# Storing the result of a decode block in two transfers from two engines

## The chip, the core and the metric

The kernel runs on one core of a Trainium2 chip. The metric is the time of one execution on the device in microseconds (us), as a median of several runs; one further execution is recorded by the hardware profiler.

## What is computed

A decode step for a batch of 4 tokens with 448 features: attention over the last 1024 entries of a cache with 8 heads of keys and values and 16 of queries, then a channel MLP, each with a residual.

```python
def _A_ref(x, k_cache, v_cache, wq, wo):
    q = (x @ wq).reshape(B, Sq, Hq, Dh).transpose(0, 2, 1, 3)
    k = jnp.repeat(k_cache[:, :, Sk - W:, :], rep, axis=1)
    v = jnp.repeat(v_cache[:, :, Sk - W:, :], rep, axis=1)
    scores = jnp.einsum("bhqd,bhkd->bhqk", q, k) * (Dh ** -0.5)
    o = jnp.einsum("bhqk,bhkd->bhqd", _softmax(scores, axis=-1), v)
    return o.transpose(0, 2, 1, 3).reshape(B, Sq, Hq * Dh) @ wo

def _B_ref(x, w1, b1, w2, b2):
    y = _layernorm(x, axis=-1)
    h = _gelu(jnp.einsum("bsd,df->bsf", y, w1) + b1)
    return jnp.einsum("bsf,fd->bsd", h, w2) + b2

h = x + _A_ref(_layernorm(x), A_k_cache, A_v_cache, A_wq, A_wo)
h2 = h + _B_ref(_layernorm(h), B_w1, B_b1, B_w2, B_b2)
```

## The kernel before

The cache and the weights, some 88 MB in float32, are packed on the host into large arrays of 128 rows. SyncE loads them one after another into a ring of three slots; each slot is loaded again when TensorE has read the last of what it held. TensorE works through the heads as the loads arrive: queries from `wq`, scores against the keys, a softmax with VectorE and ScalarE, values, and the output weights. The last slots hold the weights of the MLP, `w1` and `w2`, which arrive in pieces of falling size.

No operation is issued where it is written. `Machine` (line 79) stands in for the engines and records every call as an `Op` (line 58), in the order of the program. `emit` (line 132) then works out from the parts of the tensors that each `Op` reads and writes which earlier ones it needs, drops the needs that others imply, and issues all of them with waits on semaphores, from line 165 on. In the trace every operation therefore has the line of the recorder (L75). An `Op` with `dma` set gets a semaphore of its own, `landed_i`, that its transfer raises by 16; the others count up the semaphore of their engine. Line 61 sets `dma` for whatever is on SyncE ("SP"). Line 178 ends the program: SyncE waits for the last `Op` on the list.

The end of the kernel is a straight line. The second weights' products are summed into the bank `py` by TensorE over lines 707 to 725, with VectorE and ScalarE only bringing `gT` and `pas` along; line 727 adds the residual and bias `hb` on VectorE and puts 128 rows of 128 floats into `res`; line 728 stores `res` to `out` in one transfer of 64 KB that SyncE issues. Each group of 32 rows holds a quarter of the features, and 4 rows of a group are the batch's tokens; the host picks those out.

Of the kernel before, what the change touches and what calls it, by code (L numbers as in the profile page):

```python
# [16 lines left out]
P = 128  # L17
H = P // 2
# [16 lines left out]
class Memory:  # L35


    def __init__(self, shape, psum):
        self.psum = psum
        self.row = 1 if psum else int(np.prod(shape[1:]))  # L40
        self.granules = 1 if psum else -(-shape[0] // GRANULE)
        self.wrote = np.full((self.granules, self.row), -1)
        self.read = {}
# [14 lines left out]
class Op:  # L58
    def __init__(self, engine, emit, outs, ins, own):
        self.engine, self.emit, self.outs, self.ins, self.own = engine, emit, outs, ins, own  # L60
        self.dma = engine == "SP"


class Engine:
# [14 lines left out]
class Machine:  # L79
# [52 lines left out]
    def emit(self):  # L132
        ops = self.ops
        who = [("DMA", i) if op.dma else op.engine for i, op in enumerate(ops)]
        at_start = [None] * len(ops)
        seen = {}
        waits = []
        for i, op in enumerate(ops):
            clock = dict(seen.get(op.engine, {}))
            needs = sorted(self._needs(i, op), reverse=True)  # L140
            if op.engine == "PE":
                needs = [j for j in needs if ops[j].engine != "PE"]
            taken = []
            for j in needs:
                if clock.get(who[j], -1) >= j:
                    continue
                taken.append(j)
                for key, value in list(at_start[j].items()) + [(who[j], j)]:
                    clock[key] = max(clock.get(key, -1), value)
            kept = []  # L150
            for j in taken:
                others = [k for k in taken if k != j]
                if not any(who[k] == who[j] and k > j or at_start[k].get(who[j], -1) >= j for k in others):
                    kept.append(j)
            waits.append(sorted(kept))
            at_start[i] = clock
            seen[op.engine] = clock
        waited = {j for w in waits for j in w}
        counter = {n: self.nc.alloc_semaphore(f"done_{n}") for n in self.issuer if n != "SP"}
        count = dict.fromkeys(counter, 0)  # L160
        mark = {}
        for i, op in enumerate(ops):
            marks = [mark[j] for j in waits[i]]
            issuer = self.issuer[op.engine]
            alone = op.own == "matmul" and op.ins[0].dtype == BF16
            for sem, value in marks if alone else marks[:-1]:
                issuer.wait_ge(sem, value)
            done = op.emit()
            if marks and not alone:
                done.wait_op(*marks[-1], "sem-ge")  # L170
            if op.dma:
                mark[i] = (self.nc.alloc_semaphore(f"landed_{i}"), 16)
                done.then_inc(mark[i][0], 16)
            elif i in waited:
                count[op.engine] += 1
                mark[i] = (counter[op.engine], count[op.engine])
                done.then_inc(counter[op.engine], 1)
        self.nc.sync.wait_ge(*mark[len(ops) - 1])


class Pool:
# [19 lines left out]
def block_kernel(nc, wq0, k0, wq1, l1, l2, l3, l4, l5, l6, l7, l8, k7, vo, v7, wo, w1, w2, out):  # L201
    real, nc = nc, Machine(nc)
# [53 lines left out]
    def output_weights(t):  # L256
# [6 lines left out]
        out=ident, in_=ident, compare_op=ALU.not_equal, fill=1.0, base=0, pattern=[[-1, P]], channel_multiplier=1  # L263
# [356 lines left out]
    def w1_part(a, j):  # L620
        if a < 3:
            return slice(0, P), w1t[3 if a == 2 else a][:, FQ * j : FQ * (j + 1)]
        rows = slice(H * (j // 2), H * (j // 2) + H)
        return rows, w1t[2][rows, FQ * (j % 2) : FQ * (j % 2 + 1)]
# [46 lines left out]
    for a in (0, 1, 3, 2):  # L671
        m = Q if a == 0 else B
        for j in range(4):
            rows, w = w1_part(a, j)
# [50 lines left out]
            )  # L725
    res = once.tile([P, P], F32, tag="res", name="res")
    nc.vector.tensor_add(res, py.rearrange("p i c -> p (i c)"), hb)
    nc.sync.dma_start(out, res)
    nc.emit()


# [77 lines left out]
```

## Time and profile before

| what | us |
|---|---|
| median of 3 runs | 212.09 |
| lowest and highest of them | 211.88, 212.33 |
| the profiled execution, its own time | 211.87 |
| its span, from the first to the last instruction | 210.6 |
| TensorE busy | 139.0 |
| VectorE busy | 28.8 |
| ScalarE busy | 14.4 |

All 212.09 us are one core's. The difference between the profiled execution's own time and its span, 1.27 us, lies ahead of the first and behind the last instruction of the trace. Times inside the trace are counted from the start of the span. A row of the timeline gives the start, the length, the engine, the line, the operation with what it writes and reads, how many of them are merged, and in brackets the idle time before it and what ended that. "SPq" is SyncE's queue: its rows are the issues of transfers, and a transfer goes on after its issue ends.

### The profile page before, as it was taken

The page shows a single profiled execution, that of the slowest core. Times are in us where ns is not written, and L with a number is a line of the kernel's source. Part 1 is how long each engine was busy: PE and PEld are TensorE (multiplying, and loading weights), DVE is VectorE, ACT ScalarE, POOL GpSimd, SP SyncE. Part 2 cuts the span into 40 slices and gives each one's busy share as a digit, 9 for nine tenths or more (in the row PEclk, how much of TensorE's full clock was granted, in tenths as well). Part 3 has the DMA queues.
Part 4 walks back from the last instruction along what each step waited for, and adds up shares of the span by engine and source line. Part 5 has one row for each costly group of instructions (what it writes and reads, how often), then busy time and mean ns, then how long its engine had stood idle before and what let it go on. Part 6 is the DMA issues. An engine that isn't in the chain of part 4 may idle for free.

```text
span 210.6 us, 2206 instructions
## 1 busy us (share of the span) xinstructions
PE 139.0 (66%) x984; PEld 47.2 (22%) x984; DVE 28.8 (14%) x135; ACT 14.4 (7%) x34; POOL 5.0 (2%) x17
## 2 busy tenths in 40 slices
PE   0467759621971679198359775419806999888996
PEld 0420202200220223034012222102301233224332
DVE  7210101300020011013001104000100213012320
ACT  2010000200000010020000002000100002010311
POOL 5100000000000000000000000000000000000100
PEclk9999996996799559969967999757965899999999
DMA  7999999899999999999999999999999999999993
GB/s 296 429 399 473 448 492 389 386 436 507 398 398 410 531 389 410 410 519 398 413 411 448 481 398 425 434 470 398 434 411 442 416 428 429 425 407 439 424 409 138
DMA packets 3400, 88.42 MB, mean 420 GB/s; under 512 B 512, under 2 KB 768, under 8 KB 1344
## 3 DMA queue, kind: packets, MB, share of 16 engines
q1 hardware_dynamic: 3392, 88.30, 97.6%
q8 instruction: 7, 0.11, 0.2%
q14 instruction: 1, 0.01, 0.0%
HBM read 88.23 MB, written 0.07 MB: 419 GB/s over the span
## 4 chain that ended last, share of the span: by engine, by line
DMA 77%; PE 18%; SPq 2%; DVE 1%; issue 1%; ACT 0%
DMA slot<-l 64%; DMA slot<-w 14%; PE b_o L75 9%; PE b_s L75 4%; PE b_acc L75 3%; SPq L75 2%; PE b_m L75 1%; DVE oT L75 1%; DVE w_o L75 0%; PE b_t L75 0%; DVE o_u L75 0%; ACT o_u L75 0%; DVE o_res L75 0%
## 5 line engine op out<-in xcount | busy, mean ns | idle before, releaser
L75 PE MATMUL b_o<-slot,pT 128*32 128x512 f32 x224 | 33.6, 752 | 29.3 <-DMA slot<-l 28.5
L75 PE MATMUL b_s<-slot,qT 128*32 128x512 f32 x256 | 36.6, 722 | 10.4 <-DMA slot<-l 9.1
L75 PE MATMUL b_m<-slot,yT 128*32 128x512 f32 (+1 forms) x76 | 11.9, 734 | 11.5 <-DMA slot<-l 6.4
L75 PEld LDWEIGHTS b_o<-slot,pT 128*32 128x32 f32 x224 | 7.8, 132 | 51.4 <-DMA slot<-l 30.9
L75 PE MATMUL b_t<-idle 128*32 128x512 bf16 x64 | 18.1, 404 | 0.5 <-DVE pT L75 0.5
L75 PEld LDWEIGHTS b_s<-slot,qT 128*32 128x32 f32 x256 | 8.8, 128 | 35.9 <-issue 22.5
L75 ACT ACTIVATE o_p<-b_s,w_nm 128x512 f32<-128x512 f32 x8 | 5.4, 682 | 93.1 <-DVE w_nm L75 93.1
L75 DVE TENSOR_REDUCE w_mx<-b_s 128x1 f32<-128x512 f32 x8 | 5.5, 692 | 43.7 <-PE b_s L75 43.7
L75 DVE TENSOR_SCALAR w_o<-b_o,w_rec 128x512 f32<-128x512 f32 x4 | 3.0, 751 | 52.5 <-PE b_o L75 52.5
L75 PEld LDWEIGHTS b_m<-slot,yT 128*32 128x32 f32 x76 | 4.3, 142 | 17.9 <-DMA slot<-l 6.9
L75 PEld LDWEIGHTS b_t<-idle 128*32 128x32 bf16 x64 | 5.9, 100 | 10.3 <-issue 5.8
L75 DVE TENSOR_REDUCE w_sm<-b_m 128x32 f32<-128x128 f32 x4 | 1.2, 291 | 48.2 <-PE b_m L75 48.2
L75 PE MATMUL b_t<-ident,o_p 128*128 128x128 f32 x32 | 5.0, 285 | 4.0 <-ACT o_p L75 3.9
L75 PE MATMUL b_acc<-slot,oT 128*32 128x448 f32 x52 | 6.1, 545 | 1.9 <-DVE oT L75 1.9
L75 ACT COPY w_qs<-b_m 128x512 f32<-128x512 f32 x4 | 2.3, 584 | 60.8 <-PE b_m L75 60.8
L75 POOL TENSOR_TENSOR o_r<-w_ve,mhalf 128x1 f32<-128x1 f32 x2 | 1.1, 542 | 189.0 <-DVE w_ve L75 189.0
L75 PE MATMUL b_m<-ident,w_qs 128*128 128x128 f32 x16 | 3.5, 361 | 2.9 <-ACT w_qs L75 2.9
L75 PEld LDWEIGHTS b_t<-ident,o_p 128*128 128x128 f32 x32 | 3.4, 141 | 7.4 <-ACT o_p L75 7.4
L75 PE MATMUL b_m<-slot,mean 128*128 128x12 f32 (+1 forms) x4 | 1.1, 370 | 5.6 <-DMA slot<-wq 5.6
L75 PE MATMUL b_o<-slot,yT 128*32 128x512 f32 x10 | 4.6, 594 | 0.0
L75 PE MATMUL b_m<-ident,w_o 128*128 128x128 f32 x20 | 3.3, 286 | 1.8 <-DVE w_o L75 1.8
L75 DVE COPY pT<-b_t 128x16 f32<-128x16 f32 x32 | 3.3, 167 | 6.0 <-PE b_t L75 6.0
(94 smaller groups left out, 66.7 us busy)
## 6 DMA issues: line engine op xcount, KB each, us to landing
slot<-l SPq DMA_DIRECT2D x6, 7936.0 KB, 43.0
slot<-l SPq DMA_DIRECT2D x2, 6144.0 KB, 34.1
slot<-k SPq DMA_DIRECT2D x1, 4864.0 KB, 15.9
slot<-vo SPq DMA_DIRECT2D x1, 4544.0 KB, 33.1
slot<-k SPq DMA_DIRECT2D x1, 4096.0 KB, 43.5
slot<-v SPq DMA_DIRECT2D x1, 3072.0 KB, 19.0
slot<-w SPq DMA_DIRECT2D x1, 2240.0 KB, 28.6
slot<-w SPq DMA_DIRECT2D x1, 1792.0 KB, 34.0
```

The lines of the kernel that those rows point to most:

```text
L75: self.machine.add(Op(self.name, lambda: getattr(issuer, what)(*args, **kwargs), outs, ins, what))
```

## The change

The result is stored in two transfers of 64 rows each, the first issued by SyncE and the second by ScalarE. So that the recorder handles a transfer on ScalarE, `dma` is set by the operation's name and no longer by its engine, and the end of the program waits for every transfer that writes a tensor which the recorder doesn't hold in its own memory, which is `out` alone, in place of the last operation.

```diff
@@ class Op
-        self.dma = engine == "SP"
+        self.dma = own == "dma_start"
@@ Machine.emit
-        self.nc.sync.wait_ge(*mark[len(ops) - 1])
+        for i, op in enumerate(ops):
+            if op.dma and op.outs[0].tensor.name not in self.memory:
+                self.nc.sync.wait_ge(*mark[i])
@@ block_kernel
-    nc.sync.dma_start(out, res)
+    for queue, rows in ((nc.sync, slice(0, H)), (nc.scalar, slice(H, P))):
+        queue.dma_start(out[rows], res[rows])
     nc.emit()
```

## Rows read from the trace of the kernel before

**Rows 1.** The page: the span, and the chain that ended last by engine.
```profile
span 210.6 us, 2206 instructions
...
DMA 77%; PE 18%; SPq 2%; DVE 1%; issue 1%; ACT 0%
```

**Rows 2.** The timeline of all engines, from 200 us on.
```profile
206.89 0.53 ACT L75 COPY o_u<-b_acc 128x448 f32<-128x448 f32 x1 [2.19 <-PE b_acc L75]
...
207.85 0.73 PE L75 MATMUL b_o<-slot,gT_last 128*4 128x64 f32 x24
208.66 0.29 DVE L75 TENSOR_TENSOR o_res<-b_o,o_hb 128x128 f32<-128x128 f32 x1 [4.31 <-PE b_o L75]
208.97 0.35 SPq L75 DMA_DIRECT2D out<-o_res  x1
```

**Rows 3.** Waits of SyncE's queue: us in total, times, longest.
```profile
SPq L75 <- DVE o_res L75: 23.8, 1, 23.8
SPq L178 <- DMA out<-o_res: 1.2, 1, 1.2
```

**Rows 4.** DMA, 208.97 to 210.6: packets; queue; issue, KB, us to landing.
```profile
DMA packets 144, 0.07 MB, mean 40 GB/s; under 512 B 16, under 2 KB 144, under 8 KB 144
...
q1 hardware_dynamic: 144, 0.07, 14.2%
...
out<-o_res SPq DMA_DIRECT2D x1, 64.0 KB, 1.5
```

**Rows 5.** Windows at the end: length, busy by engine, clock, DMA share, GB/s.
```profile
208.00:208.30 0.30, 0.30 (x22) 0.15 (x11) 0.00 (x0) 0.00 (x0) 0.00 (x0) 1.00 0.00 0
...
209.75:209.80 0.05, 0.00 (x0) 0.00 (x0) 0.00 (x0) 0.00 (x0) 0.00 (x0) 1.00 0.00 0
209.80:209.85 0.05, 0.00 (x0) 0.00 (x0) 0.00 (x0) 0.00 (x0) 0.00 (x0) 1.00 0.28 72
...
209.95:210.00 0.05, 0.00 (x0) 0.00 (x0) 0.00 (x0) 0.00 (x0) 0.00 (x0) 1.00 1.09 317
...
210.15:210.20 0.05, 0.00 (x0) 0.00 (x0) 0.00 (x0) 0.00 (x0) 0.00 (x0) 1.00 0.01 0
```

**Rows 6.** The timeline of SyncE's queue: start and length of issues.
```profile
0.73 0.39 SPq L75 DMA_DIRECT2D slot<-wq  x1
...
1.64 0.82 SPq L75 DMA_DIRECT2D wq_last<-wq  x1
...
126.03 0.33 SPq L75 DMA_DIRECT2D slot<-k  x1
...
170.53 0.45 SPq L75 DMA_DIRECT2D slot<-w  x1
...
171.02 0.45 SPq L75 DMA_DIRECT2D slot<-w  x1
```

**Rows 7.** Windows at the start of the kernel, columns as in rows 5.
```profile
1.50:1.70 0.20, 0.00 (x0) 0.00 (x0) 0.17 (x2) 0.20 (x1) 0.20 (x2) 1.00 0.00 0
1.70:1.90 0.20, 0.00 (x0) 0.00 (x0) 0.17 (x2) 0.20 (x1) 0.20 (x3) 1.00 2.38 402
```

**Rows 8.** The chain that ended last, in order of time: start, us, what.
```profile
202.27 0.49 DVE o_u L75
202.76 0.02 issue
202.79 0.43 ACT o_u L75
```

**Rows 9.** Lines 178 and 800: count, ns min/median/max, first and last start.
```profile
L178 SPq EVENT_SEMAPHORE  x1: 17/17/17, 210.5 to 210.5; - x1
...
L800 ACTq DRAIN  x1: 8/8/8, 0.1 to 0.1; - x1
...
L800 ACTq EVENT_SEMAPHORE  x1: 17/17/17, 0.7 to 0.7; - x1
```

## The prediction

> **What bounds the kernel now.** I read the shares of the chain that ended last first: waiting for loads is 77% of the span and TensorE 18%, while VectorE's last operation has a share too small for a whole per cent [rows 1]. The change touches none of the loads, so the second thing to read is only the end of the timeline. It says that the store is the last piece of serial work: the last matmuls of `py` run until 208.63 us, the add into `res` runs from 208.66 to 208.95, and SyncE issues the store from 208.97 to 209.32 [rows 2]. The waits of SyncE's queue give the rest: 1.2 us at the last wait, until the store has landed [rows 3], and the DMA view gives 1.5 us from issue to landing, so to about 210.47 of a span of 210.6 [rows 4]. Nothing overlaps this tail: no engine is busy in it, and the loads were over before it, since the DMA engines stand at 0.00 from 208.0 to 208.3 [rows 5].
>
> The tail from 208.97 thus splits into four stretches, which the change can only touch one by one. The issue takes 0.35 us. From its end at 209.32 nothing moves until 209.80, which is 0.48 us of preparation. The data move from 209.80 to 210.15, which is 0.35 us [rows 5]. From there to the landing is 0.32 us without data, and 0.1 us remains to the end of the span. In the data stretch the 144 packets are 128 rows of 512 bytes and 16 small ones [rows 4]; the sixteen DMA engines are busy for 14% of 1.63 us on the mean, 0.23 us each, which is 26 ns for each of an engine's nine packets. The stretch is 0.12 us longer than that because the engines do not start together.
>
> **The change part by part.** The edit of `Op` changes no wait of an older operation: until now every operation on SyncE was a `dma_start` and every `dma_start` was on SyncE, so the old test and the new one pick the same ones, and no load, matmul or copy is moved. I cost it at nothing, and nothing needs to hide it.
>
> What is removed is one issue of 128 rows on SyncE; what is added is one of 64 rows on SyncE and one of 64 rows on ScalarE. Both wait for the same add, which ends at 208.95. ScalarE has been idle since its copy of `pas` ended at 207.42 [rows 2], so nothing of its own is in the way, and nothing is queued behind the new instruction that anyone waits for. Its start after a VectorE result is shown: an operation of VectorE begins at 202.27 and takes 0.49, and ScalarE starts 0.02 to 0.03 us after it ends [rows 8], as fast as SyncE does at 208.97. So both issues begin together.
>
> The length of an issue is not set by bytes: single transfers with the engine undisturbed cost 0.33 us for megabytes and 0.35 us for this store of 64 KB [rows 2, 6]. No plain issue of 64 rows is in the trace. From below, it could cost half, 0.17 us less. From above, it could cost what the small transfers into `wq1_last` cost, 0.82 us, which is 0.47 us more [rows 6]; those read their source in a shape of several pieces, and the half of `out` is as plain as the whole. I take no change, by the rows at 0.33 and 0.35.
>
> Two issues that are close in time are dearer. Where SyncE issues one transfer right behind another, each takes 0.45 us and the starts are 0.49 us apart, from 170.53 to 171.02 [rows 6]. The 0.10 us over 0.35 may be the price of a generator of descriptors that is still at the one before; whether two engines pay it is not in the trace. The bounds are 0, if each has a generator of its own, and a whole pitch of 0.49, if one has to wait for the other. I take 0.10, the nearest thing that the rows show for neighbours.
>
> ScalarE has issued no transfer before, so its queue is used for the first time. SyncE's own first use is in the trace: it issues from 0.73 in 0.39 us, and data move only after 1.70 [rows 6, 7], 0.97 us after the start against 0.83 for the store. That is 0.14 us of a cold start, perhaps 0.24, as the window that shows it is 0.2 us wide. ScalarE's half would start 0.14 us later, but it is only half: a DMA engine then has five packets from SyncE, 0.13 us, and five from ScalarE that arrive as those end, 0.13 us. It ends 0.14 + 0.13 = 0.27 us after its first packet against 0.23 today, so 0.04 is left. The 16 further small packets that a second transfer brings are in this.
>
> A rule of the Trainium skill speaks against the edit here: "DMA: Bandwidth & Descriptors", in its rules for kernel authors, says not to bother splitting a transfer into partition halves, because both halves spread over the same sixteen DMA engines; use one transfer of 128 partitions. The data stretch agrees as far as it goes, since the mean share passes 0.9 in its middle [rows 5], and by the rule alone the sum would have no gain and no loss in the data.
>
> Last, SyncE waits twice at the end in place of once. A wait that is already met costs 17 ns [rows 9]; it lies on the end only if ScalarE's half is first to land, or adds its decoding. I take 0.02 us, between 0 and 0.1.
>
> **The sum.** 0 for the issue, 0.10 for the neighbour, 0.04 for the cold queue and the packets, 0.02 for the wait: +0.16 us. The profiled execution took 211.87 us, of which 210.6 are the span and 1.27 lie around it; ScalarE already takes part in what brackets the kernel at its head [rows 9], so I leave that 1.27 as it is. No row shows what a second queue would do there; the nearest number is the 1.27 itself, and its doubling is left in the part outside my range. 211.87 + 0.16 = 212.03. The profiled execution is 0.22 us below the median of 212.09, so on that scale the forecast is 212.25 us, 0.08% above.
>
> **The rivals.** *A gain:* both halves are prepared side by side, an issue of 64 rows costs 0.17 us less, and the 0.12 us by which the engines start unevenly shrink to nothing. That is 0.29 us at most, 211.80 on the median's scale. For it speaks that the 0.48 us before the first packet is preparation, some of which may go by the row; against it, that 0.33 us is paid for megabytes as for kilobytes [rows 6].
>
> *One after the other, the slower side:* the two engines share one generator of descriptors, and ScalarE's issue stands behind SyncE's in full. The place is the 0.35 us issue at 208.97; the price is the pitch of 0.49 us [rows 6], plus the cold start of 0.14, less about 0.12 of data, since only half of the rows is left to be moved: +0.51, or 0.35 + 0.14 - 0.12 + 0.02 = +0.39 if the wait is the bare issue. That gives 212.48 to 212.60. It takes the time past the bound of 0.2% once ScalarE's issue stands 0.38 us or more behind (0.38 + 0.14 - 0.12 + 0.02 = 0.42 us); ScalarE's record would then be 0.73 us or longer, or begin late. For it speaks the neighbour's 0.45; against it, that this is only 0.10 more. The Trainium skill has this as a rule: "Perfetto Trace Analysis", on the DMA instruction of the hardware generator, says that the generator is shared by the sequencers that use it and is locked for exclusive use during an issue. No row of this kernel shows two engines issuing, so the trace neither bears it out nor denies it. The same would be seen if the change did not do what it says and both halves went through SyncE's queue.
>
> *A slow issue on ScalarE:* the engine pays the 0.82 us of the dearest unstalled issue [rows 6], +0.47, with the cold start and less of data +0.51: 212.60 again, and 212.8 if the neighbour's 0.10 and the wider cold start come on top. Only rows of SyncE stand for it.
>
> **How the numbers follow.** About 0.2%, or 0.42 us, is what a measurement of this kernel can tell from no change: the runs shown spread from 211.88 to 212.33. So faster means under 211.67 and slower over 212.51. The forecast has 0.57, the gain 0.20, one after the other 0.16, the slow issue 0.07. The gain's full size stays 0.13 us short of the bound, so only the spread of the runs takes it past: 0.08 of its 0.20, and 0.02 of the forecast's 0.57. The other two lie about at the upper bound: 0.09 and 0.05 of them are past it, and 0.03 of the forecast. That makes 0.10 faster, 0.73 the same, 0.17 slower. The range goes from the gain's 211.80 less half of the runs' spread, 211.6, to the slow issue's 212.8.
>
> **What would show it.** The profile after should have a second hardware queue with 80 of 160 packets; a transfer record on ScalarE's queue that begins at the add's end plus 0.02 us and lasts 0.35 to 0.45 (about 0.7 or late: one after the other; over 0.8 alone: slow issue); data over within 0.4 us; and 1.65 to 1.8 us from the add's end to the landing of the later half. An issue near 0.17 us would be the gain. If anything ahead of 208.6 us has moved by more than the usual jitter, or the time around the span is not 1.27, the prediction is wrong in a place that I haven't priced.

## The result, and the profile after

| | before | after |
|---|---|---|
| median, 8 runs each, us | 211.94 | 212.62 |
| lowest and highest, us | 211.86, 212.33 | 212.51, 212.83 |
| profiled execution, us | 211.87 | 212.64 |
| its span, us | 210.6 | 211.3 |

The ratio is 1.003, with a 95% interval of 1.0021 to 1.0039: the change makes the kernel slower by 0.3%, 0.68 us of the medians. That lies just past the 0.2% at which the prediction set its border.

In the profile after, the page names a second hardware queue; columns are packets, MB and share of sixteen DMA engines.

```profile
q1 hardware_dynamic: 3328, 88.26, 97.2%
...
q10 hardware_dynamic: 80, 0.03, 0.1%
```

The timeline of the end answers to [rows 2]:

```profile
208.80 0.29 DVE L75 TENSOR_TENSOR o_res<-b_o,o_hb 128x128 f32<-128x128 f32 x1 [4.32 <-PE b_o L75]
209.11 0.56 SPq L75 DMA_DIRECT2D out<-o_res  x1
209.12 0.56 ACTq L75 DMA_DIRECT2D out<-o_res  x1
```

The DMA view of the same end answers to [rows 4] (issue, KB, us from issue to landing):

```profile
out<-o_res SPq DMA_DIRECT2D x1, 32.0 KB, 1.9
out<-o_res ACTq DMA_DIRECT2D x1, 32.0 KB, 2.2
```

Both engines start together, 0.02 to 0.03 us after the add, as forecast. But each issue takes 0.56 us where the whole store's took 0.35, and the landings come after 1.9 and 2.2 us instead of 1.5. The two profiled executions differ by 0.77 us (211.87 and 212.64), with 1.3 us around the span in both. Of the 0.77, 0.14 lie ahead of the end of the add (208.95 and 209.09). In the single executions recorded below, whose operations ahead of the last add are the same, that add ends anywhere from 208.86 to 209.25 us, so those 0.14 are within the spread of single executions. The other 0.63 us lie behind the add, in the tail; that is about the 0.68 us by which the medians differ.

The windows at the moment when data begin to move, columns as in [rows 5]:

```profile
210.25:210.30 0.05, 0.00 (x0) 0.00 (x0) 0.00 (x0) 0.00 (x0) 0.00 (x0) 1.00 0.00 0
210.30:210.35 0.05, 0.00 (x0) 0.00 (x0) 0.00 (x0) 0.00 (x0) 0.00 (x0) 1.00 0.39 82
```

Read in such slices, SyncE's 80 packets go from 210.30 to just past 210.60, and ScalarE's 80 from there to just past 210.90. This is the DMA view of the one slice in which they meet, 210.60 to 210.65, by queue:

```profile
q10 hardware_dynamic: 8, 0.00, 43.5%
q1 hardware_dynamic: 1, 0.00, 1.1%
```

So two things are to be explained: SyncE's first packet comes 1.19 us after its issue starts, and no longer 0.83; and ScalarE's come 0.29 us behind those (210.31 and 210.60, in slices of 0.01 us). The two, 0.36 and 0.29 us, less the 0.05 by which a half's data are shorter than the whole's (0.30 against 0.35), make 0.60 of the 0.63 us.

### The profile page after: what moved, and what is told of

Read it like the earlier page. It is cut to its first block, busy times and chain, and to the rows that moved or that the text cites. A ratio compares the mean times of both kernels' runs of the same rounds, so it can differ in the third digit from the quotient of the medians.

```text
span 211.3 us, 2207 instructions
## 1 busy us (share of the span) xinstructions
PE 136.8 (65%) x984; PEld 47.0 (22%) x984; DVE 28.8 (14%) x135; ACT 14.4 (7%) x34; POOL 5.0 (2%) x17
## 4 chain that ended last, share of the span: by engine, by line
DMA 78%; PE 17%; SPq 2%; DVE 1%; issue 1%; ACT 0%
DMA slot<-l 64%; DMA slot<-w 14%; PE b_o L75 9%; PE b_s L75 3%; PE b_acc L75 3%; SPq L75 2%; PE b_m L75 1%; DVE oT L75 1%; DVE w_o L75 0%; PE b_t L75 0%; DVE o_u L75 0%; ACT o_u L75 0%; DVE o_res L75 0%
## 5 line engine op out<-in xcount | busy, mean ns | idle before, releaser
L75 PE MATMUL b_s<-slot,qT 128*32 128x512 f32 x256 | 35.1, 698 | 12.2 <-DMA slot<-l 10.9
L75 PE MATMUL b_m<-slot,yT 128*32 128x512 f32 (+1 forms) x76 | 11.3, 702 | 12.1 <-DMA slot<-l 6.9
```

The source lines that it names most:

```text
L75: self.machine.add(Op(self.name, lambda: getattr(issuer, what)(*args, **kwargs), outs, ins, what))
```

## The experiments

Three accounts were tested first: that the two engines hinder each other only when they issue at once (S), that ScalarE's queue is slow by itself (C), and that a transfer of 64 rows is dear whoever issues it (H).

**Half a store alone, by SyncE.** In place of the two transfers:

```diff
-    for queue, rows in ((nc.sync, slice(0, H)), (nc.scalar, slice(H, P))):
-        queue.dma_start(out[rows], res[rows])
+    nc.sync.dma_start(out[:H], res[:H])
```

> Only the upper 64 rows are stored, by SyncE; the lower 64 rows of the result are left out. It shows what a half costs alone. Theory S (SyncE and ScalarE share one generator of descriptors, and a half is dear only when the other engine issues at the same moment): the issue record is 0.35 us or a little less, as for 128 rows, not the 0.56 of the changed kernel; the first packet about 0.83 us after the issue starts, landing at 1.4 to 1.5 us; total 211.8 to 212.0, at or just below the kernel before. Theory C (ScalarE's queue is slow by itself, and SyncE's half is only dragged along): the same as S here. Theory H (64 rows are a dear form by themselves): issue 0.56 us, first packet about 1.2 us after it starts, landing 1.9 us, total 212.2 to 212.4.

The timeline of its end:

```profile
209.06 0.56 SPq L75 DMA_DIRECT2D out<-o_res  x1
```

Its DMA view:

```profile
out<-o_res SPq DMA_DIRECT2D x1, 32.0 KB, 1.9
```

The first packets are in the slice of 0.02 us from 210.26, 1.20 us after the start. The total is 212.28 us, ratio 1.0012 (1.0003 to 1.0022): half of the bytes, one engine, nobody beside it, and slower than the whole store. S and C fall as explanations of the longer issue; H stands.

**Half a store alone, by ScalarE.** In place of the same two lines:

```diff
+    nc.scalar.dma_start(out[H:], res[H:])
```

> Only the lower 64 rows are stored, by ScalarE; the upper 64 rows of the result are left out. Theory S: like the upper half alone on SyncE, issue 0.35 us, landing 1.4 to 1.6 us, total 211.8 to 212.1. Theory C (ScalarE's queue is slow by itself or by being used for the first time): issue 0.5 us or more, first packet 1.2 us or more after it starts, landing 1.9 to 2.2 us, total 212.3 to 212.6. Theory H: as C here.

The timeline of its end:

```profile
208.99 0.53 ACTq L75 DMA_DIRECT2D out<-o_res  x1
```

Its DMA view:

```profile
out<-o_res ACTq DMA_DIRECT2D x1, 32.0 KB, 1.9
```

The first packet is 1.17 us after the start, the total 212.31 us, ratio 1.0011 (1.0002 to 1.002). It is level with SyncE's half.

**The whole store, by ScalarE.** In place of the same two lines:

```diff
+    nc.scalar.dma_start(out, res)
```

> The whole store of 128 rows in one transfer, issued by ScalarE. Theory S: nobody else issues, so it costs what it cost on SyncE: issue 0.35 us, landing 1.5 us, total 211.9 to 212.1, within 0.1% of before. Theory C: issue 0.5 us or more, landing 1.9 to 2.2 us, total 212.3 to 212.6, and most of the change's loss stands here with no split at all. Theory H: as S.

The timeline of its end:

```profile
208.96 0.37 ACTq L75 DMA_DIRECT2D out<-o_res  x1
```

Its DMA view:

```profile
out<-o_res ACTq DMA_DIRECT2D x1, 64.0 KB, 1.6
```

The total is 211.94 us, ratio 0.9996 (0.9986 to 1.0007): nothing is lost by issuing from ScalarE. The first packet is 0.88 us after the start, against 0.83 on SyncE, and this is the queue's only use. C is out, and a first use costs 0.05 us or less.

**Both halves, by SyncE.** The second transfer changes its engine:

```diff
-    for queue, rows in ((nc.sync, slice(0, H)), (nc.scalar, slice(H, P))):
+    for queue, rows in ((nc.sync, slice(0, H)), (nc.sync, slice(H, P))):
```

> Both halves are issued by SyncE, one behind the other, with no second queue. Theory S: the first issue 0.35, the second 0.45 and 0.49 us or less behind it in start; the first half lands at 1.4 to 1.5 us, the second 1.9 to 2.0 us after the first issue starts, so total 212.3 to 212.5: between before and the changed kernel, since the halves go one after the other here too but neither slows the other's issue. Theory C: the same, and the difference of the changed kernel to this one would be ScalarE's. Theory H: both issues 0.56 us and a landing of the second past 2.4 us, total 212.8 or more.

The timeline of its end:

```profile
209.04 0.56 SPq L75 DMA_DIRECT2D out<-o_res  x1
...
209.64 0.59 SPq L75 DMA_DIRECT2D out<-o_res  x1
```

The total is 213.02 us, ratio 1.0047 (1.0032 to 1.0063). The issues stand end to end and the halves' first packets are 0.63 us apart (slices of 0.01 us from 210.24 and 210.87). On two queues they were 0.29 apart, so the second engine saves 0.34 us against two halves on one queue. What it can't do is to make up for having halves.

**What in a half is dear.** Behind the kernel before and its store, SyncE issues a row of further transfers, each when the last one has landed, so that each is alone. Two kernels did this, in one recorded execution each; the source of the first is:

```diff
     nc.sync.dma_start(out, res)
     nc.emit()
+    wide = out.rearrange("(a b) c -> a (b c)", b=2)
+    moves = [(out[:n], res[:n]) for n in (112, 96, 64, 32, 16)]
+    moves += [(wide, rs[:H, : 2 * P]), (out[:, :H], res[:, :H])]
+    moves += [(junk[:n], k7[:n, :P]) for n in (H, P)]
+    moves += [(out[H:], res[H:]), (out, res)]
+    after = real.alloc_semaphore("after")
+    for i, (dst, src) in enumerate(moves):
+        real.sync.dma_start(dst, src).then_inc(after, 16)
+        real.sync.wait_ge(after, 16 * (i + 1))
```

> The kernel before, and behind its store eleven further transfers by SyncE, each issued when the one before has landed, so that nothing overlaps: stores of 112, 96, 64, 32 and 16 rows of 512 bytes, of 64 rows of 1024 bytes, of 128 rows of 256 bytes, loads of 64 and of 128 rows of 512 bytes, the lower 64 rows, and the whole of 128 rows again. The total is some 25 us longer for that and means nothing. H1 (only a transfer of 128 rows is issued the cheap way): 0.33 to 0.37 us of issue and the first packet 0.83 us after its start for every form of 128 rows, load or store, 512 or 256 bytes; 0.5 us or more and 1.17 us for all the others, 112 rows too. H2 (it goes by the rows that each of the sixteen DMA engines gets): a rising cost from 112 over 96, 64, 32 to 16 rows, 112 close to 0.37. H3 (it goes by the bytes of the transfer): 64 rows of 1024 bytes cheap like the whole, 128 rows of 256 bytes dear like a half.

The second kernel has other forms in the list:

```diff
+    parts = [slice(0, n) for n in (80, 48, 60, 44, 72, 63)]
+    parts += [slice(Q, Q + H), slice(0, P, 2), slice(0, H), slice(0, P)]
+    moves = [(out[part], res[part]) for part in parts]
+    moves.insert(8, (out[:H, :16], res[:H, :16]))
```

> The kernel before, and behind its store eleven further stores by SyncE, each issued when the one before has landed: of 80, 48, 60, 44, 72 and 63 rows of 512 bytes, rows 32 to 95, every second row (64 of them), 64 rows of 64 bytes, the upper 64 rows, and all 128. The total is some 20 us longer and means nothing. N64 (the number 64 itself): issue 0.5 us or more and a first packet 1.12 to 1.2 us after the start for the four stores of 64 rows, wherever they begin, in steps of two too and with 64 bytes, and 0.31 to 0.36 and 0.80 to 0.84 us for the others. N4 (four rows for each of the DMA engines that take part): 60 rows as four on fifteen and 44 as four on eleven would be as dear as 64. NP (the region of the memory): rows 32 to 95 and every second row would differ from the upper half.

Timeline of SyncE's queue in the first kernel: the stores of 96, 64 and 32 rows, the 64 rows of 1024 bytes, the 128 rows of 256 bytes, and the load of 64 rows.

```profile
212.20 0.32 SPq L737 DMA_DIRECT2D out<-o_res  x1
213.74 0.56 SPq L737 DMA_DIRECT2D out<-o_res  x1
215.65 0.31 SPq L737 DMA_DIRECT2D out<-o_res  x1
...
218.47 0.50 SPq L737 DMA_DIRECT2D out<-rs  x1
...
220.46 0.35 SPq L737 DMA_DIRECT2D out<-o_res  x1
221.97 0.53 SPq L737 DMA_DIRECT2D o_junk<-k  x1
```

And in the second: 63 rows, rows 32 to 95, every second row, and 64 rows of 64 bytes.

```profile
218.03 0.28 SPq L736 DMA_DIRECT2D out<-o_res  x1
219.45 0.62 SPq L736 DMA_DIRECT2D out<-o_res  x1
221.37 0.52 SPq L736 DMA_DIRECT2D out<-o_res  x1
223.19 0.48 SPq L736 DMA_DIRECT2D out<-o_res  x1
```

All of them together, each transfer measured once unless the row says otherwise, with the first packet from the start of the issue, read in slices of 0.02 us:

| transfer | issue, us | first packet, us |
|---|---|---|
| store of 128 rows (4 times) | 0.33 to 0.37 | 0.82 to 0.84 |
| 128 rows of 256 bytes | 0.35 | 0.84 |
| 112, 96, 80, 72 rows | 0.35, 0.32, 0.35, 0.30 | 0.84, 0.80, 0.84, 0.76 |
| 63, 60, 48, 44 rows | 0.28, 0.33, 0.32, 0.29 | 0.74, 0.80, 0.80, 0.76 |
| 32, 16 rows | 0.31, 0.32 | 0.80, 0.80 |
| upper 64 rows (twice), lower 64 rows | 0.56, 0.47, 0.48 | 1.20, 1.10, 1.12 |
| rows 32 to 95 | 0.62 | 1.26 |
| every second row, 64 of them | 0.52 | 1.16 |
| 64 rows of 1024 bytes, of 64 bytes | 0.50, 0.48 | 1.16, 1.14 |
| load of 128 rows | 0.36 | 0.98 |
| load of 64 rows | 0.53 | 1.32 |

H1 and H2 both fall: 112 and 96 rows are as cheap as 128, and 16 as cheap as 112. H3 falls with the 64 rows of 1024 bytes, which are 64 KB and dear. N4 falls with 60 and 44 rows: they moved 15 and 11 small packets beside their rows, where 64 rows moved 16, which fits four rows each on fifteen and eleven DMA engines, and both are cheap. Four rows on each of all sixteen are 64 rows and can't be told apart from them. NP falls as well: rows 32 to 95 and every second row are dear like the rest. N64 holds, though its bounds were narrower than what came (64 rows from 0.47 us of issue, other counts from 0.28). What is left is the number 64 itself: every transfer of 64 rows takes 0.47 us or more to issue where no other store took over 0.37, and has its first packet at least 0.26 us later than the others, wherever the rows lie, loads as well as stores, from 64 bytes a row to 1024. The nearest counts that were tried, 63 and 72 rows, don't pay it.

**A store of 112 rows.** Nothing of the result is in the last 16 rows.

```diff
-    nc.sync.dma_start(out, res)
+    nc.sync.dma_start(out[:112], res[:112])
```

> One store by SyncE of the upper 112 rows; the lower 16 hold no token and are left out. H1: it loses the cheap way, issue 0.5 us or more, landing 1.9 us, total 212.2 to 212.4 though it moves an eighth less. H2 and H3: issue 0.35 to 0.40 us, landing 1.45 to 1.6 us, total 211.9 to 212.1.

Issue 0.36 us, landing 1.6 us, total 212.07 us, ratio 1.0008 (0.9999 to 1.0018). It is cheap like the whole and gains nothing by an eighth less of data.

**The split by columns.**

```diff
-    for queue, rows in ((nc.sync, slice(0, H)), (nc.scalar, slice(H, P))):
-        queue.dma_start(out[rows], res[rows])
+    for queue, cols in ((nc.sync, slice(0, H)), (nc.scalar, slice(H, P))):
+        queue.dma_start(out[:, cols], res[:, cols])
```

> Two transfers again, one by SyncE and one by ScalarE at the same moment, but split by columns: each has all 128 rows and 256 bytes of each, and so the same bytes as the halves of 64 rows. H1 and H2: each issue 0.35 to 0.40 us, SyncE's first packet 0.83 to 0.9 us after its start, ScalarE's packets behind SyncE's by the stretch of one transfer, 0.30 to 0.35 us, landing 1.5 and 1.85 us: total 212.2 to 212.4, +0.3 us over before and some 0.35 us under the changed kernel, as only the queueing behind one another is left. H3: 0.55 us of issue and a landing of 2.2 us as in the changed kernel, total 212.6. If the two generators worked side by side, ScalarE would land with SyncE and the total would be that of before, 211.95.

The timeline of its end:

```profile
208.89 0.35 SPq L75 DMA_DIRECT2D out<-o_res  x1
208.90 0.38 ACTq L75 DMA_DIRECT2D out<-o_res  x1
```

Its DMA view:

```profile
out<-o_res SPq DMA_DIRECT2D x1, 32.0 KB, 1.6
out<-o_res ACTq DMA_DIRECT2D x1, 32.0 KB, 1.7
```

The same bytes in the same two transfers, with 128 rows in each: 212.09 us, ratio 1.001 (1.0001 to 1.002), less than was expected. The issues are cheap again and go side by side, and the first packets are 0.11 us apart (slices of 0.01 us from 209.73 and 209.84). The two queues' packets overlap, as the DMA view from 209.90 to 209.95 shows by queue:

```profile
q10 hardware_dynamic: 26, 0.01, 66.5%
q1 hardware_dynamic: 19, 0.00, 46.5%
```

So two transfers at once are not served wholly one after the other.

**Rows, but not 64.** The border of the change is moved, to 96 and 32 rows and to 80 and 48; and beside the latter, on the same chip, the changed kernel once more. The edit for 80 and 48:

```diff
-    for queue, rows in ((nc.sync, slice(0, H)), (nc.scalar, slice(H, P))):
+    for queue, rows in ((nc.sync, slice(0, 80)), (nc.scalar, slice(80, P))):
```

> The split into two transfers from two engines at the same moment, but of 96 and 32 rows in place of 64 and 64. Theory N (a transfer of exactly 64 rows is dear, and the split into rows on two engines is not): issues of 0.32 to 0.38 us, SyncE's first packet 0.80 to 0.85 us after its start, ScalarE's 0.1 us later, landings 1.5 to 1.7 us, total 211.9 to 212.1, about 0.5 us under the changed kernel. Theory S2 (two transfers of rows of 512 bytes at once hinder each other, which those split by columns did not show): issue or landing as in the changed kernel, 1.9 and 2.2 us, total 212.5 to 212.7.

> The changed kernel with its border moved by 16 rows: 80 rows by SyncE and 48 by ScalarE, which is as close to halves as forms go that were cheap alone. Theory N64 (the loss is the price of a transfer of exactly 64 rows, twice, and the split as such costs 0.1 to 0.3 us): issues of 0.32 to 0.40 us, SyncE's first packet 0.80 to 0.85 us after the start, ScalarE's 0.15 to 0.25 us behind it, landings 1.5 to 1.6 and 1.7 to 1.8 us, total 212.1 to 212.3, 0.3 to 0.5 us under 64 and 64 on the same chip. If the loss were that two engines move near-equal shares at once: issue 0.5 us, landings 1.9 and 2.2 us, total 212.6 like 64 and 64.

> The changed kernel itself once more, beside the one with 80 and 48 rows on the same chip. Both theories: issues of 0.53 to 0.56 us, landings 1.9 and 2.2 us, total 212.5 to 212.7. Under N64 it stands 0.3 to 0.5 us over the 80 and 48, under the other theory level with it.

The timeline with 80 and 48 rows:

```profile
209.28 0.36 SPq L75 DMA_DIRECT2D out<-o_res  x1
209.28 0.40 ACTq L75 DMA_DIRECT2D out<-o_res  x1
```

Its DMA view:

```profile
out<-o_res SPq DMA_DIRECT2D x1, 40.0 KB, 1.6
out<-o_res ACTq DMA_DIRECT2D x1, 24.0 KB, 1.8
```

| split | median, us | ratio to before, 95% interval |
|---|---|---|
| 96 and 32 rows | 212.27 | 1.0014 (1.0004 to 1.0023) |
| 80 and 48 rows | 212.30 | 1.0015 (1.0006 to 1.0024) |
| 64 and 64 rows | 212.63 | 1.003 (1.0018 to 1.0041) |

The kernel before stood at 211.99 us beside the last two. Sixteen rows more on one side and less on the other take 0.33 us off, and no run of the one kernel reaches the other's: the slowest with 80 and 48 rows took 212.46 us, the fastest with 64 and 64 took 212.55. So half of the change's loss is the number 64, and the other half, 0.31 us, stays with a split by rows that avoids it. SyncE's and ScalarE's first packets are 0.16 us apart here (slices of 0.01 us from 210.13 and 210.29), and in the 96 and 32 rows 0.17 (209.88 and 210.05).

The 96 and 32 rows missed both of their forecasts: 212.27 us lies over theory N's 212.1 and under S2's 212.5. The issues are nearly as cheap as N has them, 0.36 and 0.40 us, but ScalarE's packets lag by more than its 0.1 us, and the second landing comes after 1.8 us.

**The halves staggered.** The add in two halves, each followed by its store:

```diff
-    nc.vector.tensor_add(res, py.rearrange("p i c -> p (i c)"), hb)
-    for queue, rows in ((nc.sync, slice(0, H)), (nc.scalar, slice(H, P))):
-        queue.dma_start(out[rows], res[rows])
+    sums = py.rearrange("p i c -> p (i c)")
+    for queue, rows in ((nc.sync, slice(0, H)), (nc.scalar, slice(H, P))):
+        nc.vector.tensor_add(res[rows], sums[rows], hb[rows])
+        queue.dma_start(out[rows], res[rows])
```

> The changed kernel with its last add in two: VectorE adds the upper 64 rows, which SyncE then stores, and then the lower 64 rows, which ScalarE then stores, so that the two issues no longer start together but about 0.25 us apart. If ScalarE's packets wait behind SyncE's for what makes the descriptors (the 0.30 us lag of the changed kernel), the stagger takes that lag up: both issues still 0.5 to 0.56 us, SyncE lands 1.9 us after its issue starts and ScalarE 1.9 to 2.0 us after its own, with its first packet 1.2 us after its start in place of 1.48; the total is that of the changed kernel within 0.1 us, 212.5 to 212.7. If ScalarE's half is late for another reason, its first packet is again 1.45 us or more after its start, and the total 212.8 or more.

The timeline of its end:

```profile
209.13 0.55 SPq L75 DMA_DIRECT2D out<-o_res  x1
209.46 0.53 ACTq L75 DMA_DIRECT2D out<-o_res  x1
```

Its DMA view:

```profile
out<-o_res SPq DMA_DIRECT2D x1, 32.0 KB, 1.9
out<-o_res ACTq DMA_DIRECT2D x1, 32.0 KB, 1.9
```

ScalarE starts 0.33 us later, and its first packet is now 1.18 us after its start in place of 1.48: it lands after 1.9 us, as it does alone. So in the changed kernel ScalarE's half waited 0.30 us for something that SyncE's half held, and not for anything of its own. The total of the one execution is 212.69 us, no better: the stagger costs what it saves.

## Why the prediction was half right

The forecast was 212.25 us, +0.16 over the kernel before, with 0.73 for no change that can be measured. The time, 212.62, is in the range from 211.6 to 212.8, but the upper end of that range came from the price of a rival; and the change is slower by more than 0.2%, on the side that had 0.17. The kernel before stood at 212.09 us in the three runs that the forecast started from and at 211.94 in eight, so 0.15 us of its nearness are luck. The change itself is +0.68 us, four times the forecast's.

**The part that held.** No older operation was touched, the two issues begin together 0.02 us after the add, the second queue has 80 of 160 packets, and nothing on ScalarE stands in the way. The time around the span did not change. The record of the last wait grew from 17 to 28 ns, 0.01 us of the 0.02 that a second wait was given. The rule of the Trainium skill that was weighed there ("DMA: Bandwidth & Descriptors", rules for kernel authors: don't split a transfer into partition halves) gave the right advice. Its reason, that both halves share the DMA engines, is not all of the loss here: half of the store alone, with nothing beside it, was already slower than the whole (212.28 us). No run had a gain from a split, and the rival of a gain had no ground: a store of 16 rows has its first packet after 0.80 us and a store of 128 after 0.82 to 0.84, so preparation hardly goes by the row.

**The step that failed** is "I take no change, by the rows at 0.33 and 0.35", for the issue of 64 rows. Its rows showed that an issue doesn't go by bytes, and that was right; it was carried over to the rows of the transfer, of which no plain row with 64 was in the trace. The bounds that were written beside it, 0.17 less and 0.47 more, did hold the measured 0.56, 0.21 more. But the term was also too narrow: a dear issue has a dear preparation behind it, from 0.48 us between the issue's end and the first packet to 0.63 (209.67 to 210.30). Together that is 0.36 us until the first packet, where the sum had 0. The signs that hung on it failed with it: the data were over after 0.6 us and not within 0.4, and the later half landed 2.2 us after the add and not after 1.65 to 1.8.

**The neighbour's 0.10** was near the right size for cheap forms, by luck. It was read from issue records that were 0.10 us longer one behind the other; on two engines the records hardly grew (ScalarE's 0.38 and 0.40 us against 0.37 alone), and what came late were the packets, by 0.11 us for two transfers of 128 rows and 0.16 for 80 and 48. For two of 64 it is 0.29, so this term too was thrown off by the form.

**The cold queue's 0.04** rested on a cold start of 0.14 us read from SyncE's first load. ScalarE's only store of 128 rows showed 0.05 at most against SyncE's 0.83. The load of 128 rows behind the kernel had its first packet after 0.98 us on a queue that had been in use all along: what I had put down to a first use is the difference of a load to a store.

**The rival "one after the other"** came nearest in time, 212.48 to 212.60, but not by its mechanism. It said that ScalarE's record would be 0.73 us or longer, or begin late; the record is 0.56 us, the same as SyncE's and 0.03 more than alone, and it begins on time. What goes one after the other are the packets, 0.29 us apart and not a pitch of 0.49. The rule of the Trainium skill that was named beside it ("Perfetto Trace Analysis", on the DMA instruction of the hardware generator: shared and locked during an issue) is borne out in part at most. Two dear issues ran side by side for 0.55 us, so the records do not show the lock. The second half's packets begin as the first half's end, which a lock could explain, but those of two cheap issues overlap; what held them back is not shown.

**The rival "a slow issue on ScalarE"** was as near in time, 212.60. It fails by its sign: ScalarE's record is not over 0.8 us, SyncE's is as long, and the whole store from ScalarE took 0.37 us to issue and cost nothing.

**The forecast against the runs.** 0.16 us of sum was meant for a split with nothing else dear in it. The split by columns, which is that, stands at +0.16 by the medians (212.09 against 211.93), and the split of 80 and 48 rows at +0.31. That the former agrees is partly luck: its interval goes from nothing to 0.2%, it moves 288 packets and not 160, and of the sum's terms only the 0.10 has a counterpart of its size in the traces. The number 64 accounts for the other 0.33 us.

**What stays open.** Why 64 rows are dear was not settled: neither the place, the step between rows, the bytes nor the direction change it, four rows for each DMA engine are not dear on fewer than sixteen, and no run looked at what is sent to the generator. Nor is it shown what ScalarE's half waits for. Whether a split by rows costs more than one by columns, 0.31 us against 0.16, is open: the intervals of the two overlap, and from the start of the issue to the end of the profiled execution the columns took 0.18 us more than the kernel before, 96 and 32 rows 0.25, and 80 and 48 rows 0.27. No version tried beats the kernel before.

## What to carry to other kernels

The store at the very end of this kernel is a string of costs, 0.35 us of issue, 0.48 of preparation and some 0.3 until it is confirmed, around 0.35 us of data: splitting it over two engines halved none of the first three and added a wait behind the other half. Before a form of transfer is put into a sum, its own row is needed; where the trace has none, the price of a neighbouring form is a guess, and the bounds beside it count for more than the value. And where a transfer must be cut, try the cut a few rows off from 64: 80 and 48 rows were 0.33 us cheaper here than 64 and 64.

## What the runs showed of the hardware that was not expected

Issued alone, a transfer of exactly 64 rows took 0.47 to 0.62 us to issue from SyncE or ScalarE and had its first packet after 1.10 to 1.32 us; ten other counts of rows from 16 to 112, and 128, took 0.28 to 0.37 us and 0.74 to 0.88 us for stores, and the load of 128 rows 0.36 and 0.98. Two stores that were issued by two engines at the same moment had their first packets 0.11 to 0.17 us apart in cheap forms and 0.29 in the dear one, while the same two dear halves from one engine were 0.63 us apart.
